# Re-planned PSUM banks, drain order and kv position in a one-core attention-plus-mixer kernel

## Chip, cores, metric

One core of a Trainium2 chip; each batch of runs was made on one chip, with the kernel before run beside the others. The metric is the device time of one execution in microseconds (us). Every kernel that was run was run in the same way, each run fast or slow; the times, ratios and stage lengths compared below are those of fast runs only. A ratio is the mean time of one kernel's fast runs over the mean of the other's in the same rounds, so it is not quite the ratio of the medians that are quoted beside it.

## The reference, cut

The input x (2048 tokens, 448 columns) is normalised once (LN1) and goes through two branches whose outputs are added.

```python
xn = layernorm(x)
# branch A: linear attention, 16 heads of 28
q, k, v = split(xn @ wqkv)
phi_q = concat(softmax(q @ w_phi), softmax(-(q @ w_phi)))
phi_k = concat(softmax(k @ w_phi), softmax(-(k @ w_phi)))
o = (phi_q @ (phi_k.T @ v)) / (phi_q @ sum(phi_k))
A = o @ wo
# branch B: mixer and MLP
h  = gelu(layernorm(xn) @ w1)
hs = shift_four_column_groups(h) @ w2
x1 = xn + hs
B  = x1 + gelu(layernorm(x1) @ w3) @ w4      # this layernorm is LN2
out = xn + A + B
```

## The kernel before

Instructions are recorded in program order, and each engine plays its own part of that order. A recorder works out the semaphores from the bytes (SBUF) or banks (PSUM) that each instruction touches. So the place of a line matters in two ways: it sets the order on its engine, and it sets which wait stands in front of what. Two lines that share neither an engine nor data can change places in the text without changing anything.

PSUM is used as four pairs of banks, numbered 0 to 3. A "pair" product is computed in two halves, since the contraction is packed on the upper and lower 64 rows of the PE array: the first half writes bank 0 from the low rows and bank 1 from the high rows, the second half the other way round. To "empty" or "drain" a pair means that ACT or DVE reads the finished product out of it, after which PE may write there again.

The prologue transposes 12 of the 16 token tiles on PE (`xn_T`) and four by DMA (`xn_Td`). In the excerpt of its order, `V` and `W` are the V and W1 products and `FO` the products that fold w_phi into the weights:

```python
def xn_T(i, b):
    t = pairs[b][:, :].bitcast(BF16).rearrange("p (h x) -> p h x", h=2)[:, :, 0:256]
    for kc in range(KC):
        for h, (lo, hi) in enumerate((LO, HI)):
            R.tr(t[:, h, 64*kc:64*kc+64], xn[lo:hi, i, 128*kc:128*kc+128], ident[lo:hi, lo:hi])
    R.act(xnT[:, :, 128*i:128*i+128]..., t..., ACT.Copy)          # ACT empties the bank

# ... excerpt of the order in which the prologue is played; V, W: (pair, half); v_out, w1_out: drains
W(0, 2, 0), (xn_T, 5, 2), W(0, 0, 1), (xn_T, 6, 2), W(0, 2, 1), (xn_T, 7, 3), (w1_out, 0, 0, 0),
# ...
W(1, 0, 0), (xn_T, 8, 2), W(1, 2, 0), (xn_T, 9, 2), W(1, 0, 1), (xn_T, 10, 2), (v_out, 6, 3), W(1, 2, 1), (xn_T, 11, 2),
(w1_out, 1, 0, 0), (w1_out, 1, 2, 1), V(8, 0), V(10, 0), V(8, 1), (v_out, 8, 3), V(10, 1),
# ...
FO(0, 0, 1), FO(0, 2, 0), W(3, 0, 1), (w1_out, 3, 0, 0), W(3, 2, 1), (w1_out, 3, 2, 2), FO(0, 2, 1)
```

Then come eight K/Q steps, each for two K tiles and one Q pair, with a W2 or V pair between:

```python
for ps in range(8):
    # ... k, q, w: pair products on PSUM pairs 1, 0 and 2
    k[0]()
    w[0]()
    k[1]()
    for s in range(2):
        k_exp(2 * ps, 1, s)                 # ACT empties pair 1
    if ps > 1:
        kv_tile(2 * ps - 4)                 # PE: phi_k.T @ v, K tiles of two steps ago
        kv_tile(2 * ps - 3)
    q[0]()
    w[1]()
    if kind == "w":
        w2_out(i, 2)                        # DVE empties pair 2, adds into x1
    # ... v_out
    q[1]()
    # ... q_exp
    if ps > 2:
        g_apply(ps - 3)                     # POOL: LN2
        g_T(ps - 3)                         # SP: DMA transpose into gT
    k_norm(2 * ps)                          # DVE: row sums, 1/x; POOL: phik *= 1/sum
    if kind == "w" and i < 8:
        w2_norm(i)                          # DVE: LN2 statistics; POOL: 1/sqrt every fourth tile
```

After the loop, the W3 pairs `a(p)`, `b(p)` (the two halves of one product), the last W2 pairs, kv, num tiles `N(i)` and the final products `f(n, k)` are played in a fixed list. (A num tile is phi_q times kv for one token tile. `K` are kv tiles; `kv_copy` and `kv_blocks` bring kv out of PSUM and build from it `kvq`, which the num tiles read; `A` is LN2 on POOL, `G` its DMA transpose into `gT`, which W3 reads; `S` stores.)

```python
play([
    A(5, 6, 7), G(5, 6, 7),
    a(0), (wl[12][0],), b(0), a(1), (w2_last, 12), b(1), K(12, 13),
    a(2), (wl[14][0],), b(2), a(3), (w2_last, 14), b(3),
    K(14, 15), (kv_copy,), a(4), a(5), b(4), (kv_blocks,), b(5),
    a(6), N(0), # ...
    a(8), b(8), f(2, 0), # ...
    a(26), a(27), b(26), N(14), b(27), f(1, 6), S(10, 11), N(15), f(2, 6), f(3, 6), # ...
```

The softmax here doesn't subtract the row's maximum and nothing guards it: scores larger than these inputs give would overflow.

## Time and profile before

| | before |
|---|---|
| time, median of the first 3 runs | 182.65 us (182.49 to 182.86) |
| span of the profiled run | 180.8 us, clock 1.0 |
| busiest engine | PE 173.3 us |

Two lines of the page of the kernel before: busy us of each engine with its share of the span, and the chain of work that ended last by engine.

```profile
PE 173.3 (96%) x2198; PEld 100.1 (55%) x2198; DVE 112.6 (62%) x282; ACT 82.7 (46%) x92; POOL 95.7 (53%) x140
...
PE 74%; DVE 10%; POOL 6%; DMA 4%; ACT 2%; issue 2%; ACTq 0%; DVEq 0%
```

PE looks full. It is not: the ends of matmuls are modelled, so a late start shows only partly as idle time. The better reading is from start to start. In undisturbed stretches a paired 64x512 matmul starts every 107.8 ns and a 64x448 one every 94.4 ns. The eight W2/V matmuls at 53.22 below take 1.16 us until the next group starts at 54.38, against 8 x 94.4 ns = 0.76: 0.40 us lost, of which the bracket shows 0.23.

From the timeline of PE of the kernel before (start us, length us, engine, line, operation, out<-in, shapes, count, and in brackets the idle time before it with what ended it):

```profile
20.14 0.85 PE L203 MATMUL bank<-xnT,w 64*112 64x512 bf16 x6
21.09 0.29 PE L207 MATMUL bank<-ident,xn 64*128 64x64 bf16 x8
21.21 0.85 PE L203 MATMUL bank<-xnT,w 64*112 64x512 bf16 x6
22.16 0.29 PE L207 MATMUL bank<-ident,xn 64*128 64x64 bf16 x8
22.88 2.82 PE L203 MATMUL bank<-wv,xnT 64*128 64x448 bf16 x28 [0.43 <-ACT vaug L211]
...
29.78 1.07 PE L203 MATMUL bank<-xnT,w 64*112 64x512 bf16 x8 [0.42 <-ACT hT L211]
...
34.85 0.93 PE L203 MATMUL bank<-w,hT 64*128 64x448 bf16 x8 [0.48 <-ACT hT L211]
...
53.22 0.35 PE L203 MATMUL bank<-wv,xnT 64*128 64x448 bf16 x1
53.79 0.93 PE L203 MATMUL bank<-wv,xnT 64*128 64x448 bf16 x7 [0.23 <-DVE xn L215]
54.38 0.91 PE L203 MATMUL bank<-wpk,xnT 64*128 64x448 bf16 x6
...
73.31 1.04 PE L203 MATMUL bank<-gT,w 64*128 64x512 bf16 x8 [0.37 <-DMA gT<-g_tok]
...
83.34 2.54 PE L203 MATMUL bank<-gT,w 64*128 64x512 bf16 x21
...
86.99 1.04 PE L203 MATMUL bank<-gT,w 64*128 64x512 bf16 x8 [0.25 <-ACT phik L211]
87.87 0.40 PE L203 MATMUL bank<-kvq,eq_lo 64*128 64x64 bf16 x16
...
166.72 0.92 PE L203 MATMUL bank<-wo,xnT 64*128 64x448 bf16 x8
167.71 2.82 PE L203 MATMUL bank<-w,phik 64*128 64x448 bf16 x28
```

The last two lines show one of the two places where the halves of one product follow each other: the last 8 matmuls of the first half take 0.99 us until the second half starts, against 0.76 us at the usual spacing, so 0.23 us are lost without a bracket. The four xnT tiles that come by DMA are issued on SP here (timeline of SP, same columns), and the last of them landed at 29.58, 0.2 us before the W1 group at 29.78:

```profile
21.92 6.44 SPq L218 DMA_TRANSPOSE xnT<-xn  x4
```

POOL's normalisation of the two K tiles of step 3 (timeline of POOL, kernel before) runs from 55.75 to 59.10, and the kv tiles that read them stand at 59.66, so it is never waited for:

```profile
55.75 3.35 POOL L215 TENSOR_TENSOR phik<-phik,rks 128x896 bf16<-128x896 bf16 x2
```

And the chain of waits of the kernel before leads into the first W3 matmul like this (start us, length us, what):

```profile
64.79 3.35 POOL phik L215 x2
...
69.82 0.75 POOL g_tok L215
70.58 0.02 issue
70.59 2.36 DMA gT<-g_tok
72.96 0.35 issue
73.31 12.58 PE bank L203 x171
```

The last transposed LN2 tile sits behind POOL's K normalisation of step 5. The DMA takes 2.36 us from issue to landing. (The Trainium skill, "DMA: Bandwidth & Descriptors", section "Anatomy of one DMA — SWDGE (gpsimd) path", gives a fixed cost of about 2.0 us per DMA. That was measured on another path; the 16 gT transposes here have a median of 2.5 us in the trace's DMA view, and the measured one is used.)

### The profile page before, as it was taken

Reading aid. Unit: us, or ns where it says so; the run is one execution under the profiler, and the core shown is the slowest. Engines: PE = TensorE matmul, PEld = TensorE weight load, DVE = VectorE, ACT = ScalarE, POOL = GpSimd, SP = SyncE. Lnnn points to the kernel's source line nnn. Section 1 sums busy time; section 2 is a strip of 40 time slices with the busy share of each in tenths; the row PEclk is TensorE's granted clock in tenths of the full one; section 3 lists DMA queues with packets and bytes.
Section 4 is the critical chain, followed back from the end, with each engine's and each line's share of the span. In section 5 each row is a group of like instructions: output and inputs, shape, how many; then the busy total and the mean of one; then the engine's idle time right before and its main releaser. Section 6 shows DMA issues by size and latency. Waiting matters only on the chain.

```text
span 180.8 us, 5080 instructions
## 1 busy us (share of the span) xinstructions
PE 173.3 (96%) x2198; PEld 100.1 (55%) x2198; DVE 112.6 (62%) x282; ACT 82.7 (46%) x92; POOL 95.7 (53%) x140
## 2 busy tenths in 40 slices
PE   7899999899999999999999999999999999999993
PEld 5475456656578876466445454555545545555451
DVE  5799844759799697825565983741545416465521
ACT  2368674789778777843822422422224212224000
POOL 3656860008699989980066849472450622623740
PEclk9999999999999999999999999999999999999999
DMA  5999057992001111112011351322613220311331
GB/s 168 340 210 103 2 66 181 381 377 79 0 4 29 33 29 32 30 33 58 4 29 33 60 91 29 83 80 58 91 29 83 54 59 0 83 29 29 83 88 43
DMA packets 32981, 14.87 MB, mean 82 GB/s; under 512 B 24704, under 2 KB 32448, under 8 KB 32960
## 3 DMA queue, kind: packets, MB, share of 16 engines
q1 hardware_dynamic: 30192, 12.64, 30.7%
q10 hardware_dynamic: 2768, 1.92, 3.4%
q8 instruction: 17, 0.28, 0.7%
q14 instruction: 4, 0.03, 0.1%
HBM read 7.08 MB, written 1.84 MB: 49 GB/s over the span
## 4 chain that ended last, share of the span: by engine, by line
PE 74%; DVE 10%; POOL 6%; DMA 4%; ACT 2%; issue 2%; ACTq 0%; DVEq 0%
PE bank L203 74%; DVE xn L215 3%; DVE st L215 3%; DMA xtok<-in_A_x_dram 3%; POOL rs L215 2%; POOL phik L215 2%; DVE ksum L215 2%; DMA gT<-g_tok 1%; DVE mv L215 1%; ACT hT L211 1%; POOL mv L215 1%; DVE rks L215 1%; ACT phik L211 1%; ACTq L221 0%; ACT vaug L211 0%
## 5 line engine op out<-in xcount | busy, mean ns | idle before, releaser
L211 ACT ACTIVATE phik<-bank 128x1024 bf16<-128x1024 f32 (+1 forms) x44 | 42.4, 986 | 62.0 <-PE bank L203 62.0
L203 PE MATMUL bank<-gT,w 64*128 64x512 bf16 x392 | 50.5, 377 | 0.7 <-DMA gT<-g_tok 0.4
L215 DVE TENSOR_TENSOR vaug<-bank,vaug 128x464 f32<-128x464 f32 (+3 forms) x65 | 32.6, 512 | 24.0 <-PE bank L203 22.3
L203 PE MATMUL bank<-w,phik 64*128 64x448 bf16 (+1 forms) x420 | 45.0, 349 | 0.1
L215 POOL TENSOR_TENSOR xnT<-vaug 128x196 bf16<-128x196 f32 (+1 forms) x32 | 18.0, 585 | 47.8 <-DVE vaug L215 47.8
L203 PEld LDWEIGHTS bank<-w,phik 64*128 64x128 bf16 (+1 forms) x420 | 21.7, 94 | 21.7 <-PE bank L203 0.5
L215 POOL TENSOR_TENSOR phik<-phik,rks 128x896 bf16<-128x896 bf16 x16 | 26.8, 1698 | 10.6 <-DVE rks L215 10.6
L203 PEld LDWEIGHTS bank<-gT,w 64*128 64x128 bf16 x392 | 18.4, 94 | 18.5 <-ACT phik L211 1.6
L215 POOL TENSOR_TENSOR vaug<-xn,xtok 128x448 f32<-128x448 bf16 x16 | 16.2, 1031 | 1.2 <-DVE vaug L215 1.2
L215 DVE TENSOR_REDUCE ksum<-phik 128x32 f32<-128x896 bf16 x16 | 16.8, 1048 | 0.0
L203 PE MATMUL bank<-w,hT 64*128 64x448 bf16 (+1 forms) x128 | 16.1, 350 | 0.7 <-ACT hT L211 0.5
L215 DVE TENSOR_TENSOR xn<-bank,xn 128x256 bf16<-128x256 f32 (+1 forms) x32 | 10.2, 381 | 10.1 <-PE bank L203 10.1
L203 PE MATMUL bank<-xnT,wpq 64*128 64x512 bf16 x112 | 15.7, 376 | 0.0
L203 PE MATMUL bank<-xnT,w 64*112 64x512 bf16 x112 | 15.0, 380 | 0.4 <-ACT hT L211 0.4
L215 DVE RECIPROCAL vaug<-bank 128x16 f32<-128x16 f32 x16 | 4.1, 257 | 17.9 <-PE bank L203 17.9
L203 PE MATMUL bank<-wpk,xnT 64*128 64x448 bf16 x112 | 14.7, 349 | 0.0
L203 PE MATMUL bank<-wv,xnT 64*128 64x448 bf16 x112 | 13.6, 351 | 0.7 <-ACT vaug L211 0.4
L203 PE MATMUL bank<-wo,xnT 64*128 64x448 bf16 (+1 forms) x106 | 13.4, 349 | 0.0
L215 POOL TENSOR_TENSOR rs<-mv,mhalf 128x1 f32<-128x1 f32 (+2 forms) x17 | 11.7, 689 | 1.4
L215 POOL TENSOR_SCALAR g_tok<-xn,rs 128x512 bf16<-128x512 bf16 x16 | 12.1, 768 | 0.2
L203 PEld LDWEIGHTS bank<-w,hT 64*128 64x128 bf16 (+1 forms) x128 | 8.4, 94 | 5.7 <-DVE xn L215 1.2
L211 ACT ACTIVATE xnT<-bank 128x512 bf16<-128x512 bf16 x12 | 7.2, 598 | 7.6 <-PE bank L207 7.5
(63 smaller groups left out, 180.7 us busy)
## 6 DMA issues: line engine op xcount, KB each, us to landing
w<-in_B_w_dram SPq DMA_DIRECT2D x2, 896.0 KB, 6.9
out_dram<-vaug SPq DMA_DIRECT2D x15, 112.0 KB, 1.9
w<-in_B_w_dram SPq DMA_DIRECT2D x1, 1568.0 KB, 11.8
xtok<-in_A_x_dram ACTq DMA_DIRECT2D x2, 448.0 KB, 8.5
xtok<-in_A_x_dram SPq DMA_DIRECT2D x2, 224.0 KB, 6.7
w<-in_B_w_dram ACTq DMA_DIRECT2D x2, 224.0 KB, 6.8
wo<-in_A_wo_dram SPq DMA_DIRECT2D x2, 224.0 KB, 8.3
w<-in_B_w_dram SPq DMA_DIRECT2D x1, 392.0 KB, 3.6
```

Source lines behind the costliest of these rows:

```text
L203: self.op("PE", lambda e: e.matmul(out, lhsT, rhs, start=start, stop=stop, skip_group_check=True), [out], [lhsT, rhs], tile=self._tile(lhsT))
L211: self.op("ACT", lambda e: e.activation(out, in_, func, **kw), [out], [in_] + aps)
L215: self.op(eng, lambda e: getattr(e, name)(out, *args, **kw), [out], aps)
```

## The change

The intent: let PE's transposes alternate between pairs instead of queueing for one pair that ACT has to empty each time; empty first the pair that the next product needs; put kv before the W2/V pair so that DVE has longer to empty pair 2; run LN2 sooner; and put something between the two halves of a pair product. The diff, nearly whole:

```diff
-        def xn_T(i, b):
-            t = pairs[b][:, :].bitcast(BF16).rearrange("p (h x) -> p h x", h=2)[:, :, 0:256]
-            ...
+        def xn_T(i, b, n=1):
+            t = pairs[b][:, :].bitcast(BF16).rearrange("p (h x) -> p h x", h=2)
+            for j in range(n):
+                for kc in range(KC):
+                    at = 256 * j + 64 * kc
+                    for h, (lo, hi) in enumerate((LO, HI)):
+                        R.tr(t[:, h, at:at + 64], xn[lo:hi, i + j, 128 * kc:128 * kc + 128], ident[lo:hi, lo:hi])
+            for j in range(n):
+                R.act(xnT[:, :, 128 * (i + j):128 * (i + j) + 128]..., t[:, :, 256 * j:256 * j + 256]..., ACT.Copy)
@@ LN1 of tiles 14 and 15, the DMA transposes and the later loads become ln1_end(), called from the play list
-        vps = {... ((0, 2), (2, 3), (4, 2), (6, 3), (8, 3), (10, 2))}
+        vps = {... ((0, 2), (2, 3), (4, 3), (6, 2), (8, 2), (10, 3))}
-              W(0, 2, 0), (xn_T, 5, 2), W(0, 0, 1), (xn_T, 6, 2), W(0, 2, 1), (xn_T, 7, 3), (w1_out, 0, 0, 0),
-              (w1_out, 0, 2, 1), V(4, 0), V(6, 0), V(4, 1), (v_out, 4, 2), V(6, 1), W(1, 0, 0), (xn_T, 8, 2),
-              W(1, 2, 0), (xn_T, 9, 2), W(1, 0, 1), (xn_T, 10, 2), (v_out, 6, 3), W(1, 2, 1), (xn_T, 11, 2),
-              (w1_out, 1, 0, 0), (w1_out, 1, 2, 1), V(8, 0), V(10, 0), V(8, 1), (v_out, 8, 3), V(10, 1),
-              (v_out, 10, 2, "DVE"), W(2, 0, 0), ...
+              W(0, 2, 0), (xn_T, 5, 2), W(0, 0, 1), (xn_T, 6, 3), W(0, 2, 1), (xn_T, 7, 2), (w1_out, 0, 0, 0),
+              (w1_out, 0, 2, 1), V(4, 0), V(6, 0), V(4, 1), (v_out, 4, 3), V(6, 1), (v_out, 6, 2, "DVE"), (ln1_end,),
+              W(1, 0, 0), (xn_T, 8, 3, 2), W(1, 2, 0), W(1, 0, 1), (xn_T, 10, 3, 2), W(1, 2, 1),
+              (w1_out, 1, 0, 0), (w1_out, 1, 2, 1), V(8, 0), V(10, 0), V(8, 1), (v_out, 8, 2), V(10, 1),
+              (v_out, 10, 3), W(2, 0, 0), ...
-              ... FO(0, 2, 0), W(3, 0, 1), (w1_out, 3, 0, 0), W(3, 2, 1), (w1_out, 3, 2, 2), FO(0, 2, 1)])
+              ... FO(0, 2, 0), W(3, 2, 1), (w1_out, 3, 2, 2), W(3, 0, 1), (w1_out, 3, 0, 0), FO(0, 2, 1)])
@@ K/Q steps
             k[0]()
+            if ps > 1:
+                kv_tile(2 * ps - 4)
+                kv_tile(2 * ps - 3)
             w[0]()
             k[1]()
             for s in range(2):
                 k_exp(2 * ps, 1, s)
-            if ps > 1:
-                kv_tile(2 * ps - 4)
-                kv_tile(2 * ps - 3)
@@
-            if ps > 2:
-                g_apply(ps - 3)
-                g_T(ps - 3)
             k_norm(2 * ps)
             if kind == "w" and i < 8:
                 w2_norm(i)
+            if ps > 1:
+                g_apply(ps - 2)
+                g_T(ps - 2)
@@ tail
-            A(5, 6, 7), G(5, 6, 7),
+            A(6, 7), G(6, 7),
-            a(2), (wl[14][0],), b(2), a(3), (w2_last, 14), b(3),
-            K(14, 15), (kv_copy,), a(4), a(5), b(4), (kv_blocks,), b(5),
+            a(2), (wl[14][0],), b(2), a(3), K(14, 15), b(3), (kv_copy,),
+            a(4), a(5), b(4), (w2_last, 14), (kv_blocks,), b(5),
-            a(8), b(8), f(2, 0), ...
+            a(8), f(2, 0), b(8), ...
-            ... S(10, 11), N(15), f(2, 6), f(3, 6),
+            ... S(10, 11), f(2, 6), N(15), f(3, 6),
```

More of the change, by code (lines that the diff above doesn't have):

```diff
@@ L475, in fold_pair @@
             return lambda: row_pairs(side(0, 0), side(1, 1), True), late
-        def xn_T(i, b):
-            t = pairs[b][:, :].bitcast(BF16).rearrange("p (h x) -> p h x", h=2)[:, :, 0:256]
-            for kc in range(KC):
-                for h, (lo, hi) in enumerate((LO, HI)):
-                    R.tr(t[:, h, 64 * kc:64 * kc + 64], xn[lo:hi, i, 128 * kc:128 * kc + 128], ident[lo:hi, lo:hi])
-            R.act(xnT[:, :, 128 * i:128 * i + 128].rearrange("p c (h e) -> p c h e", h=2),
-                  t.rearrange("p h (c e) -> p c h e", c=KC), ACT.Copy)
+        def xn_T(i, b, n=1):
[6 more added lines that the diff above has]
+            for j in range(n):
+                R.act(xnT[:, :, 128 * (i + j):128 * (i + j) + 128].rearrange("p c (h e) -> p c h e", h=2),
+                      t[:, :, 256 * j:256 * j + 256].rearrange("p h (c e) -> p c h e", c=KC), ACT.Copy)
         def xn_Td(i):
@@ L725, in bass_parallel_sum__linear_kernel_hedgehog__mixer_s_mlp__prompt_kernel, with ln1_two @@
         phi_blocks()
-        for i in range(10, NT, 2):
+        def ln1_two(i):
             ln1_stats(i, 2, int(i < 14))
@@ L730, in bass_parallel_sum__linear_kernel_hedgehog__mixer_s_mlp__prompt_kernel, with ln1_end @@
             ln1_apply(dve, i - 1)
-        ln1_apply(dve, 14)
-        ln1_apply(dve, 15)
-        for i in range(12, NT):
-            xn_Td(i)
-        load_rest()
-        late_3()
-        vps = {i: v_pair(i, b) for i, b in ((0, 2), (2, 3), (4, 2), (6, 3), (8, 3), (10, 2))}
+        ln1_two(10)
+        ln1_two(12)
+        def ln1_end():
+            ln1_two(14)
+            ln1_apply(dve, 14)
+            ln1_apply(dve, 15)
+            for i in range(12, NT):
+                xn_Td(i)
+            load_rest()
+            late_3()
+        vps = {i: v_pair(i, b) for i, b in ((0, 2), (2, 3), (4, 3), (6, 2), (8, 2), (10, 3))}
         wps = {(g, m): w1_pair(g, m, b) for g, m, b in ((0, 0, 0), (0, 2, 1), (1, 0, 0), (1, 2, 1), (2, 0, 0),
@@ L754, in bass_parallel_sum__linear_kernel_hedgehog__mixer_s_mlp__prompt_kernel @@
               (spin, 2, 256), V(2, 0), (v_out, 0, 2), W(0, 0, 0), (xn_T, 4, 2), V(2, 1), (v_out, 2, 3),
-              W(0, 2, 0), (xn_T, 5, 2), W(0, 0, 1), (xn_T, 6, 2), W(0, 2, 1), (xn_T, 7, 3), (w1_out, 0, 0, 0),
-              (w1_out, 0, 2, 1), V(4, 0), V(6, 0), V(4, 1), (v_out, 4, 2), V(6, 1), W(1, 0, 0), (xn_T, 8, 2),
-              W(1, 2, 0), (xn_T, 9, 2), W(1, 0, 1), (xn_T, 10, 2), (v_out, 6, 3), W(1, 2, 1), (xn_T, 11, 2),
-              (w1_out, 1, 0, 0), (w1_out, 1, 2, 1), V(8, 0), V(10, 0), V(8, 1), (v_out, 8, 3), V(10, 1),
-              (v_out, 10, 2, "DVE"), W(2, 0, 0), W(2, 2, 0), FO(1, 0, 0), W(2, 0, 1), (w1_out, 2, 0, 0), FO(1, 0, 1),
+              W(0, 2, 0), (xn_T, 5, 2), W(0, 0, 1), (xn_T, 6, 3), W(0, 2, 1), (xn_T, 7, 2), (w1_out, 0, 0, 0),
+              (w1_out, 0, 2, 1), V(4, 0), V(6, 0), V(4, 1), (v_out, 4, 3), V(6, 1), (v_out, 6, 2, "DVE"), (ln1_end,),
+              W(1, 0, 0), (xn_T, 8, 3, 2), W(1, 2, 0), W(1, 0, 1), (xn_T, 10, 3, 2), W(1, 2, 1),
+              (w1_out, 1, 0, 0), (w1_out, 1, 2, 1), V(8, 0), V(10, 0), V(8, 1), (v_out, 8, 2), V(10, 1),
+              (v_out, 10, 3), W(2, 0, 0), W(2, 2, 0), FO(1, 0, 0), W(2, 0, 1), (w1_out, 2, 0, 0), FO(1, 0, 1),
               FO(1, 2, 0), W(2, 2, 1), (w1_out, 2, 2, 1), FO(1, 2, 1), W(3, 0, 0), FO(0, 0, 0), W(3, 2, 0),
-              FO(0, 0, 1), FO(0, 2, 0), W(3, 0, 1), (w1_out, 3, 0, 0), W(3, 2, 1), (w1_out, 3, 2, 2), FO(0, 2, 1)])
+              FO(0, 0, 1), FO(0, 2, 0), W(3, 2, 1), (w1_out, 3, 2, 2), W(3, 0, 1), (w1_out, 3, 0, 0), FO(0, 2, 1)])
         def w2_norm(i):
@@ L832, in bass_parallel_sum__linear_kernel_hedgehog__mixer_s_mlp__prompt_kernel @@
         play([
-            A(5, 6, 7), G(5, 6, 7),
+            A(6, 7), G(6, 7),
             a(0), (wl[12][0],), b(0), a(1), (w2_last, 12), b(1), K(12, 13),
-            a(2), (wl[14][0],), b(2), a(3), (w2_last, 14), b(3),
-            K(14, 15), (kv_copy,), a(4), a(5), b(4), (kv_blocks,), b(5),
+            a(2), (wl[14][0],), b(2), a(3), K(14, 15), b(3), (kv_copy,),
+            a(4), a(5), b(4), (w2_last, 14), (kv_blocks,), b(5),
             a(6), N(0), (w2_norm, 8), b(6), a(7), f(1, 0), b(7), N(1), (w2_norm, 10), A(8, 9, 10, 11),
-            a(8), b(8), f(2, 0), G(8, 9), a(9), N(2), (w2_norm, 12), b(9),
+            a(8), f(2, 0), b(8), G(8, 9), a(9), N(2), (w2_norm, 12), b(9),
             a(10), f(3, 0), b(10), f(4, 0), G(10, 11),
@@ L849, in bass_parallel_sum__linear_kernel_hedgehog__mixer_s_mlp__prompt_kernel @@
             a(25), N(13), f(3, 5), b(25), f(4, 5),
-            a(26), a(27), b(26), N(14), b(27), f(1, 6), S(10, 11), N(15), f(2, 6), f(3, 6),
+            a(26), a(27), b(26), N(14), b(27), f(1, 6), S(10, 11), f(2, 6), N(15), f(3, 6),
             S(12, 13)])
```

## The prediction

> **What bounds the kernel now.** TensorE: the page gives PE 173.3 of 180.8 us busy, and PE is 74% of the chain of waits. From 94.3 to 167.7 us that chain is one PE piece. (The Trainium skill, "Trainium Kernel Development and Optimization", section Performance Expectations, warns that matmul busy time misleads because matmuls are pipelined; here start-to-start spacing shows delays that "busy" hides.) Against the steady cadence in the PE timeline (107.8 ns per paired 64x512 matmul, 94.4 per 64x448), I find about 9 us of delays, of which the change aims at these (us):
>
> - prologue, transposes waiting for ACT to empty the one PSUM pair: 0.40 (14.4), 0.09, 0.31, 0.31, and 0.61 before V at 22.9: 1.7 in all
> - 0.65 before the W1 group at 29.8; 0.74 before W2 at 34.9 (ACT hT)
> - K/Q steps, W2/V pair waiting for DVE's drain: 0.40 (53.8), 0.14 (63.4), 0.49 (68.7); 0.63 for gT at 73.3
> - 0.46 at 87.0; same-bank half after half: 0.24 (94.3), 0.23 (167.7)
>
> **What the change does.** It removes no arithmetic. POOL's and SP's streams keep their order exactly, so "LN2 sooner" should do nothing.
>
> 1. Prologue: alternating pairs and two transposed tiles per visit should remove about 1.5 us. One V drain (1.09 us) moves from the end of DVE's prologue to before LN1 of tiles 14/15. POOL cannot help with it (same page, Key Constraints: GPSIMD cannot access PSUM; none does here).
> 2. The W1 group at 29.8 also reads tiles 12-15 from DMA transposes, the last of which landed at 29.58. So its wait is DMA, not ACT as named. With LN1 of tile 15 ending near 24.2 (before 23.7) the last transpose cannot land before about 28.2; the doubled issue seen at 23.2 (2.55 instead of 1.27) overlaps an instruction fetch and may go away. I expect W1 to start near 28.8: gain 1.0, not 2.1; it now waits on DMA for about 0.9.
> 3. Draining first the W1 pair that W2 needs: gain 0.70.
> 4. kv first in K/Q steps: W2 gets 0.5 us more slack and the 0.40, 0.14 and 0.49 go. But kv now reads normalised K 1.3 us earlier. POOL's two-tile normalisation (3.35) ended at 44.11 and 59.10; kv would stand at 43.5 and 58.3. New waits on POOL: about 0.4 in step 2 and 0.95 in step 5. The gT chain (DVE drain, POOL 3.35, LN2 2.4, DMA 2.4) hangs on step 5's W2, so the wait at 73.3 grows to about 1.0. Net loss about 1.0.
> 5. W2 between b(4) and kv_blocks hides the 0.46, but its drain (1.2) goes ahead of DVE's kvq copy: num tile 0 waits about 0.55. Net -0.1.
> 6. Halves apart: gain 0.45.
>
> Sum: 1.0 + 0.7 - 1.0 - 0.1 + 0.45 = about 1.1 us.
>
> **Prediction: 181.5 us, 80% range 180.3 to 182.6.** Faster by over 2%: 0.05; within 2%: 0.94; slower: 0.01.
>
> **Right or wrong in the profile.** V(8) near 21.4 instead of 22.9; last xnT transpose lands 28.2-29.3, W1 g=3 at once after it; no wait before the first W2; new waits of kv on POOL phik in steps 2 and 5 (step 5 longest); gT wait near 1 us; a wait of num tile 0 on kvq; no gaps at the halves.
>
> **What would make it wrong.** Transposes landing earlier (gain up to 0.9 more) or stretched as before (gain gone); POOL normalising sooner than I reckon, so kv never waits (gain 1-1.5 more).

## The result, and the profile after

The changed kernel took 181.66 us (median of 4 runs, 181.33 to 181.78) against 182.69 (4 runs, 182.49 to 182.86): ratio 0.9941, 95% interval 0.9924 to 0.9958. A second measurement, after_again below, gave 0.9949 (0.9936 to 0.9962).

The same two lines of the page, changed kernel:

```profile
PE 171.8 (96%) x2198; PEld 96.0 (53%) x2198; DVE 112.1 (62%) x282; ACT 82.5 (46%) x92; POOL 95.9 (53%) x140
...
PE 70%; DVE 14%; POOL 9%; issue 2%; DMA 1%; SPq 1%; ACT 1%; DVEq 0%
```

PE has lost share on the chain of waits, and DVE and POOL have gained it: the kernel is faster and at the same time more often waiting for others. From PE's timeline of the changed kernel:

```profile
18.72 0.40 PE L207 MATMUL bank<-ident,xn 64*128 64x64 bf16 x16
18.95 1.70 PE L203 MATMUL bank<-xnT,w 64*112 64x512 bf16 x14
20.48 0.40 PE L207 MATMUL bank<-ident,xn 64*128 64x64 bf16 x16
20.72 0.83 PE L203 MATMUL bank<-xnT,w 64*112 64x512 bf16 x6
21.39 2.81 PE L203 MATMUL bank<-wv,xnT 64*128 64x448 bf16 x28
...
28.71 1.07 PE L203 MATMUL bank<-xnT,w 64*112 64x512 bf16 x8 [0.86 <-DMA xnT<-xn]
...
33.08 0.97 PE L203 MATMUL bank<-w,hT 48*128 48x448 bf16 x8
...
42.44 0.41 PE L203 MATMUL bank<-vaug,phik 64*128 64x64 bf16 x16 [0.25 <-POOL phik L215]
...
56.56 0.48 PE L203 MATMUL bank<-vaug,phik 64*128 64x64 bf16 x16
57.85 0.41 PE L203 MATMUL bank<-vaug,phik 64*128 64x64 bf16 x16 [0.81 <-POOL phik L215]
...
72.35 1.04 PE L203 MATMUL bank<-gT,w 64*128 64x512 bf16 x8 [0.69 <-issue]
...
82.90 1.69 PE L203 MATMUL bank<-gT,w 64*128 64x512 bf16 x14 [0.25 <-ACT phik L211]
...
87.44 0.41 PE L203 MATMUL bank<-kvq,eq_lo 64*128 64x64 bf16 x16 [0.36 <-DVE kvq L215]
...
165.76 0.92 PE L203 MATMUL bank<-wo,xnT 64*128 64x448 bf16 x8
166.52 0.40 PE L203 MATMUL bank<-kvq,hi 64*128 64x64 bf16 x16
166.75 2.82 PE L203 MATMUL bank<-w,phik 64*128 64x448 bf16 x28
```

The brackets of the prologue and of the first W2 pair are gone. In their place stand waits for the last DMA transpose (28.71), for POOL within the kv tiles (42.44 and 57.85: the first tile of the two runs, the second waits), a longer one before W3 (72.35), and two new ones in the tail (82.90 and 87.44). From 165.76 to 166.75 the num tile stands between the two halves, and the three follow each other without loss. The chain of waits of the changed kernel says the same of step 5:

```profile
53.71 0.77 POOL g_tok L215
54.48 3.33 POOL phik L215 x2
57.80 0.05 issue
57.85 13.81 PE bank L203 x203
```

Where the time went, from the start times of the named matmuls in the two PE timelines:

| stage | before, us | after, us | difference | predicted |
|---|---|---|---|---|
| start to V(8) | 22.88 | 21.39 | -1.49 | -1.5 |
| V(8) to W1 of the last token group | 6.90 | 7.32 | +0.42 | +0.5 |
| W1 to the K pair of step 2 | 12.96 | 12.30 | -0.66 | -0.7 |
| step 2 to the first W3 matmul | 30.57 | 31.34 | +0.77 | +1.0 |
| W3 to num tile 0 | 14.56 | 15.09 | +0.53 | +0.1 |
| num tile 0 to the start of the last matmul | 89.79 | 89.26 | -0.53 | -0.45 |
| sum | 177.66 | 176.70 | -0.96 | -1.05 |

Each stage length comes from one profiled run. How far that can be trusted shows in the runs below: with kv in its old place, the stage from step 2 to W3 took 30.35 to 30.59 us in five profiles, and the start of W1 lay anywhere from 27.92 to 28.99 us in the eight profiles that have the new prologue and W1 unaltered.

### The profile page after: what moved, and what is told of

It reads as the page before. It is cut to its first block, busy times and chain, and to the rows that moved or that the text cites. A ratio compares the mean times of both kernels' runs of the same rounds, so it can differ in the third digit from the quotient of the medians.

```text
span 179.8 us, 5076 instructions
## 1 busy us (share of the span) xinstructions
PE 171.8 (96%) x2198; PEld 96.0 (53%) x2198; DVE 112.1 (62%) x282; ACT 82.5 (46%) x92; POOL 95.9 (53%) x140
## 4 chain that ended last, share of the span: by engine, by line
PE 70%; DVE 14%; POOL 9%; issue 2%; DMA 1%; SPq 1%; ACT 1%; DVEq 0%
PE bank L203 70%; POOL phik L215 6%; DVE xn L215 5%; DVE st L215 4%; POOL rs L215 2%; DVE mv L215 1%; DMA xnT<-xn 1%; DVE vaug L215 1%; DVE ksum L215 1%; SPq L218 1%; POOL mv L215 1%; ACT phik L211 1%; POOL g_tok L215 0%; DVE rks L215 0%; DVE kvq L215 0%
## 5 line engine op out<-in xcount | busy, mean ns | idle before, releaser
L203 PE MATMUL bank<-gT,w 64*128 64x512 bf16 x392 | 50.0, 376 | 0.9 <-issue 0.7
L203 PE MATMUL bank<-w,hT 64*128 64x448 bf16 (+1 forms) x128 | 15.3, 349 | 0.0
L203 PE MATMUL bank<-wpk,xnT 64*128 64x448 bf16 x112 | 13.9, 349 | 0.0
L211 ACT ACTIVATE hT<-bank 112x1024 bf16<-112x1024 f32 x8 | 7.8, 1026 | 4.3 <-PE bank L203 4.3
```

Of the source, the lines that this page charges most:

```text
L203: self.op("PE", lambda e: e.matmul(out, lhsT, rhs, start=start, stop=stop, skip_group_check=True), [out], [lhsT, rhs], tile=self._tile(lhsT))
L211: self.op("ACT", lambda e: e.activation(out, in_, func, **kw), [out], [in_] + aps)
```

## The experiments

The parts are cut so that all of them together give back the changed kernel, text for text. The first four went in one batch on one chip, where the kernel before had a median of 182.44 us over 11 runs.

### The LN2 part alone (built, not run)

```diff
-            if ps > 2: g_apply(ps - 3); g_T(ps - 3)
             k_norm(2 * ps)
             if kind == "w" and i < 8: w2_norm(i)
+            if ps > 1: g_apply(ps - 2); g_T(ps - 2)
...
-            A(5, 6, 7), G(5, 6, 7),
+            A(6, 7), G(6, 7),
```

The built program has the same instructions in the same order on every engine as the kernel before. There was nothing to run: "half a step sooner" in the text is no sooner on any engine.

### kv_only

```diff
             k[0]()
+            if ps > 1:
+                kv_tile(2 * ps - 4)
+                kv_tile(2 * ps - 3)
             w[0]()
             ...
-            if ps > 1:
-                kv_tile(2 * ps - 4)
-                kv_tile(2 * ps - 3)
             q[0]()
```

> The kernel before with only the kv tiles moved ahead of the W2/V pair. My theory (kv now meets POOL's normalisation): the three waits of the W2/V pair (0.40, 0.14, 0.49 us) are gone, kv waits on POOL phik about 0.4 us in step 2 and 0.9 to 1.1 in step 5, the wait for gT grows from 0.63 to about 1.0; the first W3 matmul starts 0.7 to 1.0 us later than before and the time is 0.7 to 1.0 us longer (183.4 to 183.7). Rival (kv first is the gain it was meant as, up to the 1.03 us of removed waits, and the prologue gives less than it seems): the time is 0.5 to 1.0 us shorter.

Measured: 183.17 us (5 runs), ratio 1.0036 (1.0024 to 1.0048): 0.7 us longer, at the lower edge of what my theory expected; the rival that kv first is a gain falls. (The expectations recorded here give the waits on POOL in the changed kernel as 0.48 and 1.10 us. A kv tile that waits for nothing takes 0.23 us, and with that the trace gives 0.44 and 1.06; I use these.) PE's timeline of this kernel shows the two waits on POOL and the one for gT:

```profile
43.86 0.41 PE L203 MATMUL bank<-vaug,phik 64*128 64x64 bf16 x16 [0.25 <-POOL phik L215]
...
59.27 0.41 PE L203 MATMUL bank<-vaug,phik 64*128 64x64 bf16 x16 [0.80 <-POOL phik L215]
...
73.72 1.04 PE L203 MATMUL bank<-gT,w 64*128 64x512 bf16 x8 [0.64 <-DMA gT<-g_tok]
```

By start-to-start spacing they are 0.44, 1.05 and 0.99 us. From step 2 on, no W2/V pair waits longer than 0.1 us any more. Step 2 to W3 is 31.29 us against 30.57. So the part did what it was meant to do, about 1.0 us of waits removed, and paid about 1.8 us in others for it (0.44 + 1.05 + 0.99 - 0.63); the stage grew by 0.72 us.

### prologue_only

The prologue's banks and order of the changed kernel (the first half of the diff above, to the end of the play list), and the rest as before.

> The kernel before with only the prologue's new banks and order. My theory: V(8) starts at 21.4 instead of 22.9, the W1 group of the last token group at about 28.7 set by the last xnT transpose, no wait before the first W2 pair, step 2 of the K/Q loop starts 1.7 us sooner, and, as the loop and the rest are those of before, the time is 1.6 to 1.8 us shorter (180.9 to 181.1). Rival: the loop is paced by POOL and DVE rather than by PE, so that an earlier start of it is worth less than 1 us at the end.

Measured: 180.60 us (6 runs), ratio 0.9907 (0.9891 to 0.9924): 1.7 us shorter. V(8) starts at 21.84, later than expected because the input loads landed later in this profile (the fourth tile at 7.35 us instead of 6.11 in the changed kernel's); W1 at 28.99, the first W2 pair without a wait. Step 2 to W3 takes 30.41 us, as before. (That run, at 181.29 us, and one more of the six were 0.7 us slower than the other four.) The rival, that the loop swallows an earlier start, falls: the loop started 1.4 us sooner in this profile, and the last matmul 1.6 us sooner. The run takes the new banks, the moved V drain and the new drain order together; what each is worth is read from the stages of the trace and was not run alone.

### tail_only

```diff
-            a(2), (wl[14][0],), b(2), a(3), (w2_last, 14), b(3),
-            K(14, 15), (kv_copy,), a(4), a(5), b(4), (kv_blocks,), b(5),
+            a(2), (wl[14][0],), b(2), a(3), K(14, 15), b(3), (kv_copy,),
+            a(4), a(5), b(4), (w2_last, 14), (kv_blocks,), b(5),
```

> The kernel before with only kv tiles 14/15 ahead of b(3) and the second half of W2 pair 14 behind b(4). Theory after reading the trace of the changed kernel: the wait of a(6) (0.46) goes, but a(5) waits about 0.46 more for ACT's gelu of b(3), and num tile 0 about 0.5 for DVE's kvq copy: 0.4 to 0.6 us longer than before. Rival, as predicted (only the kvq wait is new): 0.1 us longer. Rival of the change: 0.4 us shorter.

Measured: 182.83 us (6 runs), ratio 1.0025 (1.0011 to 1.0038): 0.46 us longer. W3 to num tile 0 takes 15.08 us (before 14.56), the same as in the changed kernel. a(5) waits 0.46 (ACT's gelu of b(3), which now comes after kv and therefore later) and num tile 0 waits 0.53 (DVE's kvq copy), while the 0.46 at a(6) is gone. My predicted 0.1 falls: I had seen the second wait and missed the first. (The two moves of this part were not run apart; kvq_first and best2 below each take back one side.)

### halves_only

```diff
-            a(8), b(8), f(2, 0), G(8, 9), ...
+            a(8), f(2, 0), b(8), G(8, 9), ...
-            ... S(10, 11), N(15), f(2, 6), f(3, 6),
+            ... S(10, 11), f(2, 6), N(15), f(3, 6),
```

> The kernel before with only the two pair halves set apart. Theory: both PE waits on its own bank (0.24 at 94.3 and 0.23 at 167.7) go and nothing else moves: 0.4 to 0.5 us shorter. Rival (the gaps are taken up by something else there, such as DMA of oT or the h3T gelu): under 0.2 us.

Measured: 181.99 us (6 runs), ratio 0.9972 (0.9960 to 0.9984): 0.5 us shorter, both gaps gone. The second half of a pair writes the bank from the other rows, and the recorder makes PE wait for its own earlier writes there. (The Trainium skill, "PSUM — Partial Sum Buffer", section "PSUM bank collisions raise a hardware error", says that different row tiles cannot access the same bank at the same time and that software has to see to it. No run here leaves the wait out; what the trace adds is its price, 0.24 and 0.23 us when the halves touch, and nothing when 0.23 us or more of other matmuls stand between them.)

The four parts add up: -0.93, -0.28, +0.36 and +0.25 per cent make -0.60, against -0.59 and -0.51 measured for the whole.

### after_kv_late and kv_late_again

The changed kernel with kv put back to where it was:

```diff
             k[0]()
-            if ps > 1: (the two kv tiles)
             w[0]()
             ...
+            if ps > 1: (the two kv tiles)
             q[0]()
```

> The changed kernel with only the kv tiles put back behind the K exponentials, as before. My theory: the waits of kv on POOL (0.48 and 1.10) go, the W2/V pair's waits (0.40, 0.14, 0.49) come back, the gT wait falls from 1.04 to about 0.5; the time is 0.6 to 0.8 us shorter than the changed kernel's: ratio to before 0.9890 to 0.9915. Rival (with the quicker prologue kv first does pay): as long as the changed kernel or longer, 0.994 or more.

Measured: 180.99 us, ratio 0.9908 (0.9887 to 0.9928), 6 runs of which one, the profiled one, was slow (185.85 us, clock 0.951) and is left out of the ratio. Its trace is not used. So the same kernel was run again, together with the changed kernel on the same chip.

> The changed kernel itself, so that the next two have it on the same chip: 0.993 to 0.995 of before.

> The same kernel as after_kv_late, whose profile fell in a slow state. For a profile in the fast state, and against the changed kernel on the same chip. Theory: no kv wait on POOL, the waits of W2/V (0.40, 0.49) back, gT wait about 0.5, first W3 matmul 0.6 to 0.9 us sooner than in the changed kernel. Rival: no difference beyond 0.2 us.

Measured: the changed kernel 181.66 us, 0.9949 (0.9936 to 0.9962); kv late 181.04 us, 0.9923 (0.9911 to 0.9935). Kv late is about 0.5 us quicker in this batch (0.9949 - 0.9923 = 0.26 per cent). In the trace step 2 to W3 takes 30.59 us against 31.35 in the changed kernel of the same batch, 0.76 us. The waits on POOL are gone, the 0.41 and 0.49 of the W2/V pair are back, and gT is waited for by 0.65. The quicker prologue does not make kv first pay.

### after_half_pool (wrong result)

```diff
-                R.ew(pool, "tensor_tensor", ph, ph, rks[:, r, :].unsqueeze(2).to_broadcast([128, 2 * H, DH]),
+                hp = phik[:, j, :, 0:DH // 2]
+                R.ew(pool, "tensor_tensor", hp, hp, rks[:, r, :].unsqueeze(2).to_broadcast([128, 2 * H, DH // 2]),
                      op=ALU.mult)
```

> Wrong result on purpose: the changed kernel with POOL's normalisation of K over half of the columns, so that its work for two tiles falls from 3.35 us to about 1.8; everything else the same. My theory (POOL's backlog is what kv and the gT chain wait for): the kv waits in steps 2 and 5 and the gT wait nearly vanish, 2.0 to 2.6 us shorter than the changed kernel, 0.980 to 0.983 of before. Rival (DVE's row sums and drains pace these steps, and POOL is merely named as the last link): under 1 us shorter.

Measured: 179.06 us (4 runs), ratio 0.9806 (0.9788 to 0.9823): 2.5 us less than the changed kernel by the difference of the ratios to 0.9941. One tile's POOL work falls from 1.70 to 0.95 us. DVE's and ACT's work is untouched, and the chain of waits from the last W1 group (28.27) to the tail (79.21) becomes one piece of PE:

```profile
28.27 50.94 PE bank L203 x731
```

Both kv waits fall below 0.1 us and the gT wait to 0.26, and step 2 to W3 takes 29.19 us, 2.15 less than in the changed kernel; the rest of the 2.5 is about what W1 started sooner in this profile (0.44 us), which this edit does not touch. So POOL's backlog is the cause of these waits, and not DVE's sums ahead of it. (Half of K is left unnormalised here, and the comparison with the reference still passed at its tolerance; the kernel is for the timing only.)

### after_w1_other_tiles (wrong result)

```diff
-    lambda k, kc, lo, hi: xnT[lo:hi, kc, 512 * g:512 * g + 512]
+    lambda k, kc, lo, hi: xnT[lo:hi, kc, 512 * min(g, 2):512 * min(g, 2) + 512]
```

> Wrong result on purpose: the changed kernel with the last W1 group reading token tiles 8 to 11 instead of 12 to 15, which come by DMA transpose. My theory (the last DMA transpose sets its start): it starts at about 27.9 instead of 28.7, when ACT has emptied its bank, and the time is 0.6 to 0.9 us shorter than the changed kernel's. Rival (ACT's gelu of the group before holds its bank): no change.

Measured: 180.75 us (4 runs), ratio 0.9898 (0.9881 to 0.9916), about 0.8 us less than the changed kernel. The W1 group starts at 28.03 without idle time (PE's timeline of this kernel):

```profile
28.03 1.07 PE L203 MATMUL bank<-xnT,w 64*112 64x512 bf16 x8
```

In the changed kernel the DMA transposes are what holds W1; with them out of the way only 0.23 us of waiting is left there. In the kernel before it was both: W1 waited 0.65 in the profile where the last transpose landed at 29.58, and 0.23 at 29.37 in halves_only, which has the prologue of before and where it landed at 28.95.

### kvq_first

The changed kernel with DVE's kvq copy ahead of its drain of W2 pair 14:

```diff
-            a(4), a(5), b(4), (w2_last, 14), (kv_blocks,), b(5),
+            a(4), a(5), b(4), (wl[14][1],), (kv_blocks,), (w2_out, 14, 2), b(5),
```

> The changed kernel with DVE's kvq copy ahead of its drain of W2 pair 14, PE's order untouched. Theory: num tile 0 no longer waits (0.53 becomes under 0.1), 0.4 to 0.5 us shorter than the changed kernel. Rival (ACT's half of kvq or the bank is what it waits for): no change.

Measured: 180.96 us (6 runs), ratio 0.9911 (0.9897 to 0.9925), 0.7 us less than the changed kernel of the same batch. In the trace W3 to num tile 0 is 14.56 us, 0.53 less than in the changed kernel, and num tile 0 follows b(5) and a(6) at once. The remaining 0.2 us lie within the two intervals. (The profiled run, 180.28 us, is the fastest of the six: W1 had started 0.65 us sooner in it, with the same prologue code.) The wait of a(5), 0.44 us, is still there: it belongs to the other half of the edit.

```profile
84.62 1.68 PE L203 MATMUL bank<-gT,w 64*128 64x512 bf16 x14
86.13 0.40 PE L203 MATMUL bank<-kvq,eq_lo 64*128 64x64 bf16 x16
```

### best2

The diff is against the changed kernel.

```diff
-            if ps > 1:
-                kv_tile(2 * ps - 4)
-                kv_tile(2 * ps - 3)
+            if ps > 2:                          # still first, but three steps behind
+                kv_tile(2 * ps - 6)
+                kv_tile(2 * ps - 5)
...
+            if ps == 5:                         # LN2 of 6, 7 and the fourth gT transpose before POOL's K work
+                w2_norm(i)
+                g_apply(ps - 2)
+                g_T(ps - 2)
             k_norm(2 * ps)
-            if kind == "w" and i < 8:
+            if kind == "w" and i < 6:
                 w2_norm(i)
-            if ps > 1:
+            if ps > 1 and ps != 5:
                 g_apply(ps - 2)
                 g_T(ps - 2)
...
-            a(0), (wl[12][0],), b(0), a(1), ...
+            a(0), (wl[12][0],), b(0), K(10, 11), a(1), ...
-            ... a(3), K(14, 15), b(3), (kv_copy,), a(4), a(5), b(4), (w2_last, 14), (kv_blocks,), b(5),
+            ... a(3), b(3), K(14, 15), (kv_copy,), a(4), a(5), b(4), (wl[14][1],), (kv_blocks,), (w2_out, 14, 2), b(5),
```

> A version drawn from the theory: the changed kernel with kv first but three steps behind K instead of two (tiles 10 and 11 move behind b(0)), LN2 of tiles 6 and 7 and the fourth gT transpose ahead of K's normalisation in step 5, and in the tail kv 14/15 back behind b(3) and DVE's kvq copy ahead of its drain of W2 pair 14. Theory: no wait of PE longer than 0.2 us from step 2 to num tile 0; 2.0 us less than before from step 2 to the first W3 matmul, 0.45 less from there to num tile 0; with prologue and halves 4.0 to 4.7 us shorter than before: 0.974 to 0.978. Rival (POOL's total work is the limit, so the waits only move to where POOL is late next): 0.983 or more.

Measured: 178.73 us (5 runs), ratio 0.9788 (0.9771 to 0.9805): 3.75 us less than before by the medians, just short of the expected 0.974 to 0.978. It is correct and faster than both kernels; whether by over 2% the interval leaves open. Step 2 to W3 is 28.92 us, 1.65 less than before instead of 2.0, and 0.47 of that is only moved: W3 to num tile 0 is 15.03 us, 0.47 more than before where I had expected 0.45 less, since kv tiles 10 and 11 (0.47 us of PE) now stand there. The waits of a(5), a(6) and num tile 0 are gone. Two waits over 0.2 us are left that I had not expected. In step 2 the Q pair waits 0.49 us for ACT, as the chain of waits of this kernel shows (the two ACT pieces before, then PE alone for 35 us); and b(3) waits 0.32 for PE's own bank (at 78.83), since I had put it straight behind a(3), the first half of the same product.

```profile
40.73 0.81 ACT vaug L211
41.55 1.84 ACT eq_lo L211 x2
43.39 0.05 issue
43.43 35.36 PE bank L203 x532
```

### best3

The diff is against best2.

```diff
+        kv_first = {2: (0,), 3: (2, 3), 4: (4, 5), 5: (6,), 6: (7,), 7: (8, 9)}
-            if ps > 2:
-                kv_tile(2 * ps - 6)
-                kv_tile(2 * ps - 5)
+            for j in kv_first.get(ps, ()):
+                kv_tile(j)
...
+            if ps == 2:
+                kv_tile(1)
             q[0]()
...
-            ... b(1), K(12, 13), a(2), (wl[14][0],), b(2), a(3), b(3), K(14, 15), ...
+            ... b(1), a(2), (wl[14][0],), b(2), a(3), K(12, 13), b(3), K(14, 15), ...
```

> best2 with kv spread by when POOL is ready (tile 0 first and tile 1 later in step 2; 2,3; 4,5; 6; 7; 8,9 in steps 3 to 7) and kv 12/13 between the two halves of W3 pair 3. Theory: the two waits that best2 still had go (0.49 at q of step 2 on ACT, 0.33 at kv 14/15 on PE's own bank): 0.5 to 0.8 us shorter than best2, 0.974 to 0.977 of before. Rival: no better than best2 (0.979), as other waits take their place.

Measured: 178.82 us (5 runs), ratio 0.9797 (0.9783 to 0.9811): no better than best2, as the rival said. The two waits are gone (the one recorded as that of kv 14/15 was b(3)'s), but in the trace two others came: 0.32 in step 5 for ACT's Q exponentials and 0.31 in step 7 (at 66.78) for DVE's drain of the W2 pair of step 6, although two kv tiles stand in front of it there. Step 2 to W3 is 28.91 us, the same as in best2. How much cover a W2 pair needs can't be told from these two runs.

## Why the prediction was right

**The sum.** Predicted 181.5 us with a range of 180.3 to 182.6, measured 181.66: 1.0 us less than before, against the 1.1 predicted. It came about as written, with gains of 1.7 (prologue, first W2 pair, W1) and 0.5 (halves) and losses in the loop and the tail. Parts run alone confirm the signs: prologue_only 0.9907, halves_only 0.9972, kv_only 1.0036, tail_only 1.0025.

**Prologue (points 1 and 2).** V(8) at 21.39 against the predicted 21.4. The last transpose landed at 28.46 (predicted 28.2 to 29.3) and W1 started at 28.71 (predicted 28.8). The second transpose's issue on SP fell from 2.55 to 1.28 us, as held possible (the first one's rose from 1.22 to 1.53). after_w1_other_tiles showed that the transposes hold W1.

**First W2 pair (point 3).** Predicted 0.70; 0.66 from W1 to step 2. The wait is gone.

**kv (point 4).** Predicted waits on POOL of about 0.4 and 0.95, measured 0.44 and 1.06; gT wait predicted about 1.0, measured 1.04; the stage was 0.77 longer, where I had said 1.0. after_half_pool showed POOL to be the cause, kv_only and kv_late_again that the move itself is the loss. That LN2 would do nothing was settled by the built program and by the unchanged order on POOL and SP.

**Tail (point 5).** This is the term that was mis-sized: "Net -0.1", a loss of 0.1, was a loss of 0.53 in the changed kernel and of 0.46 by tail_only's time. The kvq wait came as predicted (0.53 for 0.55), shown by kvq_first. What I left out was the other half of the edit: kv 14/15 moved ahead of b(3), so ACT's gelu of b(3) started later and a(5), which reuses its pair, waited 0.44 (not at all before, where a(4), a(5) and b(4) run through from 83.34). With it the sum closes: 0.44 + 0.53 - 0.46 is 0.51. In best2, with kv 14/15 back behind b(3), a(5) does not wait.

**Halves (point 6).** Predicted 0.45; 0.53 in the stage and 0.5 in halves_only. The loop being less bad by 0.2 and the halves better by 0.1 offset most of the tail's 0.4; the total owes its closeness partly to that.

Left open in part: why the transposes' issue was stretched in the kernel before. In the four profiles with the prologue of before, a 16 KB instruction fetch started at 22.3 to 23.7 us, while the transposes were being issued, and one issue took 1.8 to 2.6 us. In the nine fast profiles with the new prologue it started at 21.0 to 21.9, and at most one issue was stretched, to 1.5. The other DMA transposes of the 13 fast traces (their DMA packets set against SP's issues) point to the fetch and not to the prologue. All 65 issues that held SP for over 1.4 us had a 16 KB fetch under way meanwhile; of the 461 issues without one, the longest took 1.34 us. (A fetch does not always stretch: 46 issues with one stayed under 1.4 us.) No run moved the fetch alone, so what set its time, and so whether the new prologue or luck moved it, is not shown.

## What to carry to other kernels

Moving work ahead of a wait on one engine also moves its reads ahead: before doing so, write down when each input is ready and how much slack it has (here 0.55 us of slack at POOL, against a move of 1.3 us). Look which engine's stream really changes: a line moved only past lines of other engines does nothing. And when a product's two halves or a drain change places, follow every later user of the same bank, since the cost turns up at the next reuse and not at the move.

## What the Trainium skill lacked or had wrong

- "PSUM — Partial Sum Buffer" (section "PSUM bank collisions raise a hardware error") says that software must keep row tiles apart in a bank, but gives no price. Here two touching halves cost 0.24 and 0.23 us (0.32 in best2), and 0.23 us or more of other matmuls between them removed it (halves_only, ratio 0.9972).
- "DMA: Bandwidth & Descriptors" (section "Anatomy of one DMA — SWDGE (gpsimd) path") splits up the fixed cost for one path, with about 50 ns for the sequencer's dispatch. For DMAs issued on SP the time for which an issue holds SP is what spaced the four xnT transposes here: 1.27 us for each transpose one after the other, 0.40 to 0.59 for nearly every plain load, and 2.3 to 2.5 us from issue to landing of a transpose when undisturbed.
- I found in no page what an instruction fetch costs the DMA transposes that it falls upon; the nearest is "Runtime: NRT & Kernel Launch" (section "Instruction fetch mechanics"), which has no figure for it. Here a 16 KB fetch took 0.9 to 1.8 us, and a transpose's issue took up to 2.9 us instead of 1.3 when one fell upon it, and never over 1.34 us without one. That it is the cause is not shown by a run that moves the fetch alone.
